# Score columns of the second stage's diagonal blocks: half blocks stacked on the two halves of the partitions

## The chip, the cores and the metric

The kernel runs on one core of a Trainium2 chip. A core has TensorE (PE in the profile; PEld is its weight load), VectorE (DVE), ScalarE (ACT), GpSimd (POOL) and SyncE (SP, which here only issues DMA transfers). They run side by side and meet at semaphores. The metric is the device time of one execution in microseconds (us); lower is better. Matmuls write to PSUM, here eight banks of 512 f32 columns on 128 partitions; DVE and ACT read PSUM, POOL does not.

## What is computed

Two stages, one after the other, on 8 batches of 448 tokens. The first is attention with a soft cap on 12 heads of width 64; its output, laid side by side, is the input x (448 x 768) of the second, four "expert" attentions with a causal mask, of which each token uses two, with weights from a gate. Cut to what matters:

```python
# stage 1, per batch and head
scores = cap * tanh(q @ k.T / 8 / cap)
x[:, head] = softmax(scores) @ v
# stage 2, per batch: 4 experts e, width 64
logits = x @ w_gate                      # the two largest of 4 are kept: w = softmax of the two
s = (x @ wq[e]) @ (x @ wk[e]).T / 8      # keys after the query are masked
out += w[e] * softmax(causal(s)) @ (x @ wv[e]) @ wo[e]
```

## The kernel before

**Stage 1** goes head pair by head pair: 48 pairs p, six to a batch, then two short passes for what is left of the last batch. Scores are held transposed, keys on the partitions. A pair's scores fill three PSUM areas one after the other, named X (three banks X0 to X2) and twice Y (banks Y0, Y1), by matmuls with 64 contraction rows (two heads, one on partitions 0 to 63, one on 64 to 127; `heads`, L854) and one with 128 rows (`tails`, L864). ACT takes each area with tanh (`tanh`, L907) and then the whole pair with exp (`expo`, L919). PE multiplies by the values (`pv`, L934, L942) into one of three banks A0 to A2, DVE normalises (L965, L968) and the result is transposed into xT, the input of stage 2 (L1019 and L1028, later pairs by a DMA transpose).

**Stage 2** of a batch is spread over the pairs of the next batch. `b_v` makes the values vB (L1088, evicted at L1083), `b_qk` queries and keys (L1096), `b_gate` and the functions after it the gate on POOL, `b_mask` the mask of the first or second choice. A half stage is a batch b and a choice s (first or second expert of each token); there are 14 of them, since the last batch has a path of its own (`last`, `last2`). In a half stage:

- `b_score` (L1282) computes the causal scores, all four experts at once: contraction over 2 x 128 rows (r = 0, 1), where the mask leaves a query's row non-zero only at its expert. Keys lie on the 128 partitions in blocks of 128 (block 3 holds only the last 64), queries on the columns. Banks X0 and X1 take 1024 columns: H0 holds the three diagonal blocks of 128 x 128 and two blocks of 64 queries, H1 what lies right of the diagonal. That is 18 matmuls with 128 rows and 128 output partitions.
- One ACT exp over both banks (L1301) writes pB, the probabilities, 1024 columns.
- `causal` (L1308) sets masked entries to zero on POOL: one operation on three diagonal blocks (L1311) and one on the 64 x 64 tail (L1318).
- `b_pv` (L1341) multiplies pB by vB for four query blocks n of 128, ten matmuls of 260 columns (L1351), in PSUM banks from A0 to A2 or X0 to X2, and DVE normalises and weighs the result into oB (L1364, L1366).

After both halves of a batch, `b_ot` adds them on POOL (L1376) and transposes them, for batches from 4 on by a DMA transpose (`turned`, L450 to L454), and `b_wo` multiplies by wo (L1413) and stores the result. The mask of the later batches goes through a DMA transpose as well (mT from mB, L1268, used at L1170).

**What sets the order.** The kernel does not issue as it goes. Each function records operations in a `Graph` with an engine, a cost, reads and writes and, for some, a due time. The order of ACT's fixed operations (tanh and exp) is written out; `solve` lists all others by due time against that clock, and each engine then issues its list in that order. `RANKS` adds hundredths of a us to the due time of single operations from a given planner time on; `TURN` is the planner's time for a DMA transpose, `SWITCH` 0.1 its price when PE goes from or to the matmuls with 64 rows (only operations named sX, sY, sL, sR count as such). Operations with `first` get ahead of others. None of these numbers is an instruction; they move instructions. Where the scores of a half stage come (`exps`), the exp of L1301 stands between two tanh steps of ACT, and the X area of stage 1 must wait for it.

Of the kernel before, what the change touches and what calls it, by code (L numbers as in the profile page):

```python
# [25 lines left out]
    (7.5, {  # L26
        136: 93, 174: 305, 290: -418,
    }),
    (27.5, {
        507: 475,  # L30
    }),
    (67.5, {
        678: -572, 692: 231, 735: -81, 738: -31, 741: 513, 841: 473, 1112: 748, 1167: -284,
    }),
    (87.5, {
        716: 497, 727: -643, 760: -112, 767: -1037, 862: 1282, 888: 375, 919: 264,
    }),
    (127.5, {
        1092: 467, 1196: 214, 1239: -453, 1249: 345, 1267: 323, 1277: 281, 1398: -60, 1401: 289,
        1405: 243, 1449: -132, 1535: 337, 1537: 820,  # L40
    }),
    (147.5, {
        1338: 97, 1345: 117, 1355: 477, 1387: -702, 1413: 186, 1525: 119, 1548: -196,
    }),
    (167.5, {
        1600: 205, 1607: 294,
    }),
# [7 lines left out]
    }),  # L55
    (254.5, {
        2520: -331, 2577: -265, 2635: -902, 2645: 2133, 2659: 128, 2667: 486, 2678: 522, 2702:
        -188, 2703: -340, 2706: -238, 2713: -937, 2729: -581, 2766: 2204, 2788: 297,
    }),
)  # L60
TWIRE = 0.1
TURN = 2.2
SAIL = 1.1
# [11 lines left out]
MD = 4  # L75
# [256 lines left out]
def kernel(  # L332
# [117 lines left out]
    def turned(n, dst, src, r, w, name, due=None):  # L450
# [34 lines left out]
    qm = [[sb(f"qm{s}_{r}", [128, S]) for r in range(2)] for s in range(2)]  # L485
    pP = [sb(f"pP{i}", [128, 2, 64 + 1024]) for i in range(2)]
    pB = [pP[i // 2][:, i % 2] for i in range(4)]
# [15 lines left out]
    qL = sb("qL", [128, 2, 128])  # L503
    vL = sb("vL", [128, E, Dh + 1])
    p2 = yp[NPV % NYP].rearrange("p a s -> p (a s)")[:, 0 : E * 512].rearrange(
        "p (e c t) -> p e c t", e=E, c=4)
# [108 lines left out]
    def setup_b():  # L615
        def pad():
            for t in yf:
                nc.gpsimd.memset(t[:, 7 * S :], 1.0)

        gp(0.5, pad, w=["ypad"], due=120.0)  # L620

        def tri_():
            nc.gpsimd.memset(tri, 0.0)
            for a in range(1, E):
                nc.gpsimd.memset(tri[:, :, a, 0:a], 1.0)

# [10 lines left out]
        def pz():  # L637
            for t in pB:
                nc.gpsimd.memset(t[:, 0:64], 0.0)

        gp(0.6, pz, w=[("pB", i) for i in range(4)])
# [110 lines left out]
    def tr(p):  # L752
# [45 lines left out]
        if p >= KD:  # L798
            pe(0, lambda: tq(g, 0, 2), [("q16", i), "ident"], [("tps", p, "q")], g, occ=0.1,
               name=f"trq{p}")  # L800
            pe(0, lambda: tq(g, 2, 4), [("q16", i), "ident"], [("tps", p, "r")], g, occ=0.1)
            def qe():
# [6 lines left out]
            dve(c_dve(S, p < NAT), qe, [("tps", p, x) for x in "qr"],  # L809
                [("qk", t, "q"), ("qkw", t)], g, name=f"qk{p}")  # L810
            return
# [313 lines left out]
    def b_v(b, ref):  # L1125
        x = b % 2
        j1 = PJ if b == LB - 1 else 0
        for n in range(4):
            g = Group(AUX + XB, 1.8)
            hr = [("half", "v", n)] if b == LB - 1 else []  # L1130
            for j0 in range(j1, NDC, 2):
# [13 lines left out]
                lambda t: t[lo:128, 0 : E * Dh].rearrange("p (e d) -> p e d", d=Dh)),  # L1145
                [("vps", b, n)] + hr, [("vB", x, n)], g, name=f"vB{b}")

    def b_qk(b, ref):
        x = b % 2
        for r in range(2):  # L1150
            for which in "kq":
# [4 lines left out]
                for j in range(j1, NDC):  # L1156
# [3 lines left out]
                               (f"w{which}2", 2 * r), (f"w{which}2", 2 * r + 1)],  # L1160
                       [(which, b, r)], g, name=f"{which}{b}_{r}",
                       due=(ref, 25.225 + 9.62 * r + 13.055 * (which == "q")))
# [80 lines left out]
    def b_mask(b, s):  # L1243
# [9 lines left out]
        if b < MD:  # L1253
            for r in range(2):
# [7 lines left out]

                pe(0, mm, [("mB", s), "ident"], [("mt", b, s, r)], g, occ=0.22, name=f"mT{b}")
                dve(c_dve(S, True), lambda g=g, r=r: nc.vector.tensor_tensor(
# [13 lines left out]
    def keys(c):  # L1278
        o = S - 128 if c == KC else 128 * c
        return slice(o, o + 128)  # L1280

    def b_score(b, s):  # L1282
        x = b % 2
        for part, bk in ((H1, "X1"), (H0, "X0")):
            for i, (o, c, q0, n) in enumerate(part):
                def mm(o=o, c=c, q0=q0, n=n):
                    ps = BANK[f"X{o // 512}"]
                    a = min(n, max(KM - q0, 0))
                    for d, m, t in ((0, a, q0 + TL), (a, n - a, max(q0 - KM, 0))):
                        for r in range(2):  # L1290
                            if m:
                                nc.tensor.matmul(  # L1292
                                    ps[:, o % 512 + d : o % 512 + d + m], kB[x][r][:, keys(c)],
                                    qm[s][r][:, t : t + m], start=(r == 0), stop=(r == 1),
                                )

                pe(0, mm, [("kB", x, r) for r in range(2)] + [("qm", s, r) for r in range(2)],
                   [("s", bk)], occ=2 * c_pe(n), name=f"sB{b}_{s}", takes=(bk,) if i == 0 else ())
        pi = 2 * (b % 2) + s
        pb = pB[pi]  # L1300
        act(c_act(1024), lambda: nc.scalar.activation(  # L1301
            pb[:, 64:], PART["X"].rearrange("p a c -> p (a c)"), AF.Exp, scale=isc),
            [("s", "X0"), ("s", "X1")], [("pB", pi)], fixed=True, name=f"eB{b}_{s}",
            frees=("X0", "X1"))
        b_score.last = fixed_last()
        causal(pb, pi, "")

    def causal(pb, pi, nm):  # L1308
        def diag():
            blk = pb[:, 128:512].rearrange("p (a c) -> p a c", a=3)  # L1310
            nc.gpsimd.affine_select(  # L1311
                out=blk, in_=blk, compare_op=ALU.is_ge, fill=0.0, base=0,
                pattern=[[0, 3], [1, 128]], channel_multiplier=-1,
            )

        def tail():
            blk = pb[64:128, 64:128]
            nc.gpsimd.affine_select(  # L1318
                out=blk, in_=blk, compare_op=ALU.is_ge, fill=0.0, base=0,
                pattern=[[1, 64]], channel_multiplier=-1,  # L1320
            )

        gp(0.6, diag, [], [("pB", pi)], name="diag")
        gp(0.25, tail, [], [("pB", pi)], name="diagt")

    def cols(n):

        res = []
        for c in range(min(n, KC - 1) + 1):
            if c == n:  # L1330
                o = 64 + H0[1 + c][0]
            elif c == 2:
                o = 64 + H0[3][0] + 64
            else:
                o = 64 + H1[c][0] + WIN[n] - 128 * (c + 1)
            res.append((c, o))
        if n == 3:
            res.append((3, 0))
        return res

    def b_pv(b, s):  # L1341
        x = b % 2
        pi = 2 * (b % 2) + s
        for n in range(4):
            g = Group(AUX + XB, 1.6)
            cs = cols(n)
            for i in range(0, len(cs), 2):
                def mm(g=g, i=i, cs=cs):
                    for t in range(i, min(i + 2, len(cs))):
                        c, o = cs[t]  # L1350
                        nc.tensor.matmul(  # L1351
                            bank(g)[:, 0 : E * (Dh + 1)], pB[pi][:, o : o + 128],
                            vB[x][:, c, :, :], start=(t == 0), stop=(t == len(cs) - 1),
                        )

                pe(0, mm, [("pB", pi), ("pB", pi, 0), ("pB", pi, 1), (b, f"mw{s}")] + [("vB", x, c) for c, _ in cs],
                   [("pvB", b, s, n)], g,
                   occ=0.11 * len(cs[i : i + 2]), name=f"pvB{b}_{s}")
            k_ = (2 * s + n) % 4
# [41 lines left out]
    def b_wo(b, ref, off, step=1.0):  # L1401
        x = b % 2
        for n in range(4 if b < LB - 1 else 3):
# [3 lines left out]
            for f in range(2):  # L1407
# [3 lines left out]
                def mm(g=g, n=n, c0=c0, c1=c1):  # L1411
# [447 lines left out]
```

## Time and profile before

| | |
|---|---|
| median of three runs | 305.21 us (304.68 to 305.82) |
| profiled execution, its time | 304.79 us |
| its span in the profile | 303.1 us |
| last two exps of stage 1 on ACT | 283.51 to 286.05 us |
| granted TensorE clock | 1.00 throughout |

Times in the profile are us from the start of its span. A timeline row gives start, length, engine, line, operation, output <- input, partitions x elements and the count of merged instructions. Matmuls overlap: a matmul of 65 columns is shown with 193 ns while the next one starts 30 ns after it. So what PE can do is read from the distance of starts, not from the length of a row.

### The profile page before, as it was taken

How to read it: one execution, taken by the hardware profiler on the slowest of the kernel's cores; microseconds unless marked ns; L12 is line 12 of the kernel's file. 1: busy time of each engine (PE TensorE's matmuls, PEld its weight loads, DVE VectorE, ACT ScalarE, POOL GpSimd, SP SyncE). 2: the span in 40 equal slices, each digit the busy share in tenths (PEclk: the TensorE clock that was granted, in tenths of full speed). 3: DMA queues.
4: the chain of work that ended last, by engine and by line, in shares of the span. 5: the costliest groups of instructions: out<-in, count | busy, mean ns of one | idle time of the engine just before them, and what ended most of it. 6: DMA issues, size and time to landing. Idle time of an engine off the chain costs nothing.

```text
span 303.1 us, 8955 instructions
## 1 busy us (share of the span) xinstructions
PE 282.0 (93%) x3470; PEld 188.1 (62%) x3470; DVE 213.5 (70%) x630; ACT 290.2 (96%) x244; POOL 189.4 (62%) x537
## 2 busy tenths in 40 slices
PE   7897989999999999999999999999898999989992
PEld 4463546666666676667666676656665675657771
DVE  3354556866867877687887887697766878486972
ACT  5999999999999999999999999999999999989981
POOL 6793435997699664958799355927469305711580
PEclk9999999999999999999999999999999999999999
DMA  6999999999993399677996874455028751743136
GB/s 168 223 206 238 236 233 298 284 225 281 264 233 88 118 257 244 161 216 194 280 197 170 235 244 123 55 151 146 2 52 123 216 92 21 103 142 93 37 151 215
DMA packets 86874, 53.12 MB, mean 175 GB/s; under 512 B 47536, under 2 KB 83120, under 8 KB 86832
## 3 DMA queue, kind: packets, MB, share of 16 engines
q1 hardware_dynamic: 86448, 52.13, 69.8%
q8 instruction: 27, 0.44, 0.6%
q10 hardware_dynamic: 384, 0.43, 0.5%
q14 instruction: 15, 0.12, 0.2%
HBM read 36.19 MB, written 11.01 MB: 156 GB/s over the span
## 4 chain that ended last, share of the span: by engine, by line
ACT 64%; PE 15%; POOL 5%; DMA 5%; DVE 5%; issue 4%; ACTq 0%; DVEq 0%; POOLq 0%
ACT yp L907 33%; ACT yp L919 28%; ACT pP L1301 3%; DMA mT<-mB 3%; PE A L1413 2%; PE X L1292 2%; PE A L1088 2%; PE Y L854 1%; DMA ktf<-in_k_dram 1%; PE A L942 1%; POOL oS L1376 1%; POOL mB L1248 1%; PE A L1479 1%; DMA oT<-oS 1%; PE A L1514 1%
## 5 line engine op out<-in xcount | busy, mean ns | idle before, releaser
L919 ACT ACTIVATE yp<-yp 128x3136 f16<-128x3136 f16 (+4 forms) x51 | 142.4, 2794 | 0.0
L907 ACT ACTIVATE yp<-Y 128x896 f16<-128x896 f32 (+2 forms) x100 | 101.7, 1017 | 1.3 <-PE Y L854 1.3
L907 ACT ACTIVATE yp<-X 128x1344 f16<-128x1344 f32 (+2 forms) x50 | 68.3, 1367 | 0.4 <-PE X L854 0.3
L942 PE MATMUL A<-v,yp 128*128 128x65 f16 x1008 | 49.8, 193 | 0.0
L942 PEld LDWEIGHTS <-yp 128*128 128x128 f16 x1008 | 43.6, 97 | 4.0 <-issue 2.1
L934 PE MATMUL A<-vtz,yp 128*128 128x130 f16 x168 | 37.3, 222 | 3.9 <-ACT yp L919 1.6
L744 POOL CAST v<-vf 128x384 f16<-128x384 f32 x48 | 24.6, 519 | 20.8 <-PE A L942 13.1
L968 DVE TENSOR_TENSOR xk<-A,rca 128x256 f16<-128x256 f32 x84 | 35.3, 421 | 2.2
L708 POOL CAST q<-qf 112x512 f16<-112x512 f32 x44 | 26.6, 618 | 13.7 <-PE A L758 9.0
L439 DVE COPY ob<-A 128x384 f32<-128x384 f32 (+1 forms) x50 | 25.6, 550 | 2.4 <-PE A L1413 2.0
L817 DVE COPY qk<-A 128x960 f16<-128x960 f16 x32 | 20.3, 652 | 9.2 <-PE A L758 9.0
L934 PEld LDWEIGHTS <-yp 128*128 128x128 f16 x168 | 16.2, 97 | 16.1 <-issue 8.8
L854 PE MATMUL Y<-qk 64*128 64x448 f16 x136 | 24.7, 357 | 1.5 <-ACT yp L907 0.9
L1366 DVE SCALAR_TENSOR_TENSOR oB<-A,rcb,mw 128x256 f16<-128x256 f32 x55 | 25.3, 477 | 1.0
L1311 POOL TENSOR_SCALAR_AFFINE_SELECT pP<-pP 128x384 f16<-128x384 f16 x14 | 7.4, 528 | 29.3 <-ACT pP L1301 29.3
L965 DVE RECIPROCAL rca<-A 128x4 f32<-128x4 f32 x84 | 15.0, 178 | 14.2 <-PE A L942 13.2
L1413 PE MATMUL A<-wo,oT 128*128 128x384 f16 x106 | 22.8, 326 | 1.0 <-DVE qm L1170 1.0
L1351 PE MATMUL A<-vB,pP 128*128 128x260 f16 x138 | 22.2, 274 | 1.3 <-DVE oB L1366 0.5
L1028 DVE COPY xT<-A 128x448 f16<-128x448 f16 (+1 forms) x38 | 14.7, 386 | 11.2 <-PE A L1019 10.8
L1088 PE MATMUL A<-wvg,xT 128*128 128x260 f16 x168 | 21.3, 274 | 0.6 <-DVE oB L1366 0.3
L1376 POOL TENSOR_TENSOR oS<-oB,oB 128x512 f16<-128x512 f16 x14 | 16.1, 1155 | 8.2 <-issue 5.0
L758 PE MATMUL A<-ident,q 112*128 112x112 f16 x192 | 19.8, 214 | 0.7 <-DVE oB L1366 0.4
(240 smaller groups left out, 620.2 us busy)
## 6 DMA issues: line engine op xcount, KB each, us to landing
qf<-in_q_dram SPq DMA_DIRECT2D x23, 448.0 KB, 5.7
kf<-in_k_dram SPq DMA_DIRECT2D x23, 384.0 KB, 5.0
vf<-in_v_dram SPq DMA_DIRECT2D x23, 384.0 KB, 4.7
out_dram<-ob SPq DMA_DIRECT2D x21, 384.0 KB, 3.1
ktf<-in_k_dram SPq DMA_DIRECT2D x46, 32.0 KB, 5.0
vtf<-in_v_dram SPq DMA_DIRECT2D x46, 32.0 KB, 4.3
out_dram<-ob SPq DMA_DIRECT2D x6, 192.0 KB, 2.9
ob<-in_moe_wv_dram SPq DMA_DIRECT2D x2, 384.0 KB, 4.8
```

The source lines that it names most:

```text
L439: (nc.scalar.copy if o.eng == "ACT" else nc.vector.tensor_copy)(dst(), src())
L708: e(q16[i], qf[s][:, h].rearrange("p h (c d) -> p c h d", c=QC))
L744: nc.gpsimd.tensor_copy(v16[u][:, :, :, 0:Dh], vf[s][:, h].rearrange("p h (c d) -> p h c d", c=KC))
L854: nc.tensor.matmul(dst[:, g, o], kT[r, 128 * (c + 1) : 128 * (c + 2)], t[r, qs], start=True, stop=True,)
L907: ACTS[what, p] = act(c_act(n * (b - a)), lambda: nc.scalar.activation(y[:, a:b, 0:n], src[:, 0 : b - a, 0:n], AF.Tanh, scale=isc / capf), ...
L919: act(c_act(n * (b - a), False), lambda a=a, b=b, n=n: nc.scalar.activation(y[:, a:b, 0:n], y[:, a:b, 0:n], AF.Exp, scale=capf), ks, ks, f ...
L934: nc.tensor.matmul(ps[:, n, :, :], y[:, 2 * S + w : 2 * S + w + 128], vtz[u], start=(n == 0), stop=False, skip_group_check=True,)
L942: nc.tensor.matmul(ps[:, n, h, :], y[:, o : o + 128], v16[u][:, h, c, :], start=False, stop=(c == 2), skip_group_check=True,)
L968: dve(c_dve(128 * m), lambda g=g, i=i, rc=rc, m=m: nc.vector.tensor_tensor(xk[p % NXK][:, 2 * i : 2 * i + m, :, :], view(g)[:, 0:m, :, 0:D ...
L1088: nc.tensor.matmul(bank(g)[:, 0 : E * Dh + E], xT[x][:, j, WIN[n] : WIN[n] + 128], wvg[:, j, :], start=(j == j1), stop=(j == jn),)
L1366: dve(c_dve(E * Dh) + 0.06, lambda g=g, k_=k_, n=n: nc.vector.scalar_tensor_tensor(oB[s][:, n, :, :], view(g)[:, :, 0:Dh], rcb[k_][:, 0, : ...
L1413: nc.tensor.matmul(bank(g)[:, 0 : D // 2], oT[x][:, n // 2, r, n % 2, :], wo2[r][:, c0:c1], start=(r == 0), stop=(r == 1),)
```

## The change

The diagonal blocks of 128 x 128 are no longer computed whole. A diagonal block has three quarters that matter: the two triangles of 64 x 64 on its diagonal and the full square above them. The square and one triangle need all keys of the block for its later 64 queries (they become part of `ROWS`, 128 partitions). The triangle of the earlier 64 queries needs only 64 keys (`HALF`): two such half blocks share 64 columns, one on output partitions 0 to 63, one on 64 to 127. Scores take 2 x 448 columns in place of 2 x 512.

```diff
-    H0 = ((0, KC, KM, 64), (64, 0, 0, 128), (192, 1, 128, 128), (320, 2, 256, 128),
-          (448, 2, KM, 64))
-    H1 = ((512, 0, 128, 320), (832, 1, 256, 192))
+    HALF = ((0, 0, 0, 0), (0, 64, KM, KM), (448, 0, 256, 256), (448, 64, 128, 128))
+    ROWS = ((64, 0, 64, 384), (512, 1, 192, 256), (768, 2, 320, 128))
...
+        its = [[("r", *y) for y in ROWS if y[0] // 448 == i] + [
+            ("h", *y) for y in HALF if y[0] // 448 == i] for i in range(2)]
+        for i in (1, 0):
+            for m_, (kind, o, c, q0, n) in enumerate(its[i]):
+                lead = m_ == 0
+                if kind == "h":
+                    row, k0, q0, n = slice(c, c + 64), q0, n, 64
+                    kk = slice(k0, k0 + 64)
+                else:
+                    row, kk = slice(0, 128), slice(128 * c, 128 * (c + 1))
...
+                    ps = PART["X"][row, i, o - 448 * i : o - 448 * i + n]
...
-        act(c_act(1024), lambda: nc.scalar.activation(
-            pb[:, 64:], PART["X"].rearrange("p a c -> p (a c)"), AF.Exp, scale=isc),
+        act(c_act(896), lambda: nc.scalar.activation(
+            pb.rearrange("p (a c) -> p a c", a=2), PART["X"][:, 0:2, 0:448], AF.Exp, scale=isc),
```

The causal mask takes three POOL operations in place of two, and the zeroed columns of pB with their four memsets go:

```diff
+        gp(0.28, lambda: keep(two[0:64, :, 0:64], [0, 2], [1, 64]), [], [("pB", pi)], name="diag")
+        gp(0.42, lambda: keep(two[64:128, :, 0:128].rearrange("p a (b c) -> p a b c", b=2),
+                              [0, 2], [0, 2], [1, 64]), [], [("pB", pi)], name="diag")
+        gp(0.2, lambda: keep(pb[64:128, 768:832], [1, 64]), [], [("pB", pi)], name="diagt")
```

The product with the values is split accordingly. A query block n below 3 gets, in place of one matmul for its diagonal block, one with 64 rows into output partitions 0 to 63 and one with 128 rows into 64 to 127; block 3 ends with one of 64 rows into 64 to 127. For n = 1 the half block lies on partitions 64 to 127 while its values lie on 0 to 63, so a DMA copies them into a new buffer vH once for each batch. The banks are now A0 to A2 alone.

```diff
+            if n == 1:
+                sp(lambda: nc.sync.dma_start(vH[x][64:128], vB[x][0:64, 1]), [("vB", x, 1)], [("vH", x)],
+                   name=f"vH{b}", lat=2.6)
...
+    def own(n):
+        return ((0, 0), (64, 448), (0, 448))[n]
...
-            g = Group(AUX + XB, 1.6)
+            g = Group(AUX, 1.6)
+            its = []
+            for c in range(min(n, KC)):
+                o = ROWS[c][0] + WIN[n] - ROWS[c][2]
+                its.append((slice(0, 128), slice(o, o + 128), slice(0, 128), vB[x][:, c]))
+            if n < KC:
+                p0, o = own(n)
+                v_ = vH[x] if n == 1 else vB[x][:, n]
+                its.append((slice(p0, p0 + 64), slice(o, o + 64), lo64, v_))
+                o = ROWS[n][0]
+                its.append((slice(0, 128), slice(o, o + 64), hi64, vB[x][:, n]))
+            else:
+                its.append((hi64, lo64, hi64, vB[x][:, n]))
...
+                        nc.tensor.matmul(
+                            bank(g)[q_, 0 : E * (Dh + 1)], pb[rows, cs], v_[rows],
+                            start=(t == 0 or len(its) == 2), stop=(t >= len(its) - 2),
+                            skip_group_check=True)
```

The planner's numbers are new: `TURN`, and a `RANKS` list of 35 tables in place of 9, most of them new. Some buffers that an eviction waited for are now named by the matmul before it, so that the planner lists that matmul later.

```diff
-TURN = 2.2
+TURN = 3.0
 RANKS = (
...
-                   [("wop", b, n, f)], g, occ=0.325, name=f"wo{b}")
+                   [("wop", b, n, f), ("ob", n, f)], g, occ=0.325, name=f"wo{b}")
...
-                   [("pvB", b, s, n)], g,
-                   occ=0.11 * len(cs[i : i + 2]), name=f"pvB{b}_{s}")
+                   [("pvB", b, s, n)] + [("rcb", (2 * s + n) % 4)] * (i == 0), g,
+                   occ=0.11 * len(its[i : i + 2]), name=f"pvB{b}_{s}")
...
```

The order of ACT's fixed operations is the same in both kernels. On the other engines the order differs from the first 20 us on. In the built programs PE has 3470 matmuls before and 3540 after; SP has seven more transfers (the copies to vH) and the same number of every other kind.

More of the change, by code (lines that the diff above doesn't have):

```diff
@@ new lines @@
+    (233.43, {
+        2252: -705, 2336: 300, 2398: 1708, 2521: 339, 2530: 192, 2582: 57, 2607: 262, 2665: 503,
+        2669: 334, 2696: -310,
+    }),
+    (83.5, {
+        608: 378, 689: 206,
+    }),
+    (189.5, {
+        1743: 794, 1831: 339,
+    }),
+    (203.5, {
+        1759: 351, 1776: 1390, 1948: 179, 2182: -495,
+    }),
+    (217.5, {
+        2160: 326,
+    }),
+    (231.5, {
+        2252: 620, 2451: 412, 2471: 180,
+    }),
+    (245.5, {
+        2328: 1111,
+    }),
+    (214.5, {
+        1776: -364, 1945: 353, 2006: 293, 2008: 240, 2051: 118, 2069: -356, 2160: 340, 2212:
+        785, 2341: 456, 2396: -451, 2471: -308, 2521: 489,
+    }),
@@ L485 @@
     qm = [[sb(f"qm{s}_{r}", [128, S]) for r in range(2)] for s in range(2)]
[L486 removed]
+    pP = [sb(f"pP{i}", [128, 2, 896]) for i in range(2)]
     pB = [pP[i // 2][:, i % 2] for i in range(4)]
@@ L504 @@
     vL = sb("vL", [128, E, Dh + 1])
+    vH = [sb(f"vH{i}", [128, E, Dh + 1]) for i in range(2)]
     p2 = yp[NPV % NYP].rearrange("p a s -> p (a s)")[:, 0 : E * 512].rearrange(
@@ L1160, in b_qk @@
                                (f"w{which}2", 2 * r), (f"w{which}2", 2 * r + 1)],
-                       [(which, b, r)], g, name=f"{which}{b}_{r}",
+                       [(which, b, r)] + ([("qm", s, r) for s in range(2)]
+                                          if which == "q" and b >= MD else []), g, name=f"{which}{b}_{r}",
                        due=(ref, 25.225 + 9.62 * r + 13.055 * (which == "q")))
```

161 lines of the change are left out of this document (92 added, 69 removed), and 13 rows, old and new, of the table RANKS.

## The prediction

> **What bounds the kernel now.** I read the page's totals first, then the waits of ACT and its timeline, then the same for PE, and last the chain.
>
> ```profile
> PE 282.0 (93%) x3470; PEld 188.1 (62%) x3470; DVE 213.5 (70%) x630; ACT 290.2 (96%) x244; POOL 189.4 (62%) x537
> ```
> ```profile
> ACT yp L907 <- PE Y L854: 1.3, 1, 1.3
> ...
> ACT pP L1301 <- PE X L1292: 0.9, 1, 0.9
> ACT yp L907 <- PE X L854: 0.3, 1, 0.3
> ```
>
> ACT is busy 96%. Once it runs (its first wait, 1.3, is at the start) it waits twice, 1.2 us together, until the last exp of stage 1. What a step of ACT costs is the distance of starts:
>
> ```profile
> 212.16 2.84 ACT L919 ACTIVATE yp<-yp 128x3136 f16<-128x3136 f16 x1
> 214.87 1.05 ACT L1301 ACTIVATE pP<-X 128x1024 f16<-128x1024 f32 x1
> 215.77 0.95 ACT L907 ACTIVATE yp<-Y 128x896 f16<-128x896 f32 x1
> 216.57 1.34 ACT L907 ACTIVATE yp<-X 128x1344 f16<-128x1344 f32 x1
> ```
>
> The score exp of 1024 columns takes 0.90 us (214.87 to 215.77), a tanh over two slices of 448 columns 0.80 us. But ACT is not alone. Windows of the whole middle, of one pair of heads, and of the end (columns: length, then busy time and count of PE, PEld, DVE, ACT, POOL, then clock, DMA share, GB/s):
>
> ```profile
> 62.00:279.00 217.00, 208.55 (x2631) 142.56 (x2631) 164.38 (x478) 215.71 (x169) 139.63 (x356) 1.00 0.66 163
> ```
> ```profile
> 85.00:90.49 5.49, 5.49 (x70) 3.67 (x71) 3.30 (x9) 5.49 (x5) 5.49 (x16) 1.00 0.88 239
> ```
> ```profile
> 279.00:303.10 24.10, 18.29 (x235) 12.87 (x234) 15.68 (x56) 16.16 (x30) 10.66 (x36) 1.00 0.38 126
> ```
>
> In the middle PE is idle for 8.45 of 217 us, in the pair shown not at all, and there ACT is full as well. So both engines are near their limit, and the question is how much PE has to spare. Its timeline around that pair:
>
> ```profile
> 84.72 0.35 PE L1096 MATMUL A<-xT,wk 128*128 128x448 f16 x1
> 85.00 0.36 PE L854 MATMUL Y<-qk 64*128 64x448 f16 x2
> 85.20 0.35 PE L854 MATMUL X<-qk 64*128 64x448 f16 x2
> 85.49 0.34 PE L1019 MATMUL A<-perm,xk 128*128 128x128 f16 x3
> 85.67 0.22 PE L1019 MATMUL A<-pswap,xk 128*128 128x128 f16 x1
> 85.72 0.54 PE L1096 MATMUL A<-xT,wk 128*128 128x448 f16 x2
> 86.10 0.61 PE L1351 MATMUL A<-vB,pP 128*128 128x260 f16 x4
> ...
> 88.23 0.34 PE L942 MATMUL A<-v,yp 128*128 128x65 f16 x6
> 88.51 0.36 PE L854 MATMUL Y<-qk 64*128 64x448 f16 x2
> 88.81 0.23 PE L934 MATMUL A<-vtz,yp 128*128 128x130 f16 x1
> ```
>
> Three things stand here. (1) Two matmuls of 64 rows on the two partition halves cost one: each L854 row is a pair, and the X pair ends 0.19 after the Y pair (85.55 after 85.36), the step of 448 columns. Steps fit columns / 2.4 GHz + 2.5 ns throughout. (2) A change from matmuls with 128 rows to such with 64 or back costs 0.105 us: L1096 ends at 85.07, the pair of 448 columns after it at 85.36, which is 0.29 and not 0.19; L942 ends at 88.57, L854 at 88.87, 0.30; back to 128 rows, the first L1019 (0.22 long) ends at 85.71, 0.16 after 85.55, where 0.055 is its step. (3) PE fills a score area as soon as ACT has freed it, so it can be late by little: the Y pair of 88.51 ends at 88.87, and ACT takes it at 89.21.
>
> ```profile
> 88.04 1.53 ACT L907 ACTIVATE yp<-X 128x1344 f16<-128x1344 f32 x1
> 89.21 1.17 ACT L907 ACTIVATE yp<-Y 128x896 f16<-128x896 f32 x1
> ```
>
> **PE's load in the middle.** I cut 62 to 279 us at the end of each first fill of an X area, 38 stretches, 216.6 us. The 2631 matmuls of the window row come to 174.8 us by the step formula (pairs of 64 rows once), the 180 changes between 128 and 64 rows at 0.105 to 18.9 us: 193.7 in all, so 23.0 us to spare (8.45 of it visible as idle; the rest lies behind the overlap of rows). It is uneven: stretches of a half stage's score have 0.6 to 2 us, those of `b_v` and `b_qk` next to none (80.0 to 85.6: 5.53 of 5.59 us).
>
> **The change, part by part.** *ACT's exp over 896 columns.* 0.90 becomes 0.80, as the tanh over the same two slices of 448: 14 x 0.105 = −1.47 us on ACT. That an access of two slices costs more than one run is excluded by that same row.
>
> *More matmuls.*
>
> ```profile
> L1351 PE MATMUL A<-vB,pP 128*128 128x260 f16 x138 | 22.2, 274 | 1.3 <-DVE oB L1366 0.5 <-DVE qk L817 0.2
> ...
> L1292 PE MATMUL X<-qm,kB 128*128 128x64 f16 x112 | 10.8, 193 | 0.2 <-DVE qm L1170 0.2
> L1292 PE MATMUL X<-qm,kB 128*128 128x128 f16 x112 | 10.6, 220 | 0.0
> ...
> L1351 PE MATMUL X2s<-vB,pP 128*128 128x260 f16 x2 | 0.4, 274 | 0.0
> ```
>
> A half stage's product with the values has 13 matmuls in place of ten; four take 0.61 with 0.274 for the last, so 0.112 each: +0.34 us, 4.7 us in all. Its scores have 20 in place of 18 with the same column sum (8 x 64 + 2 x 768 against 2 x 1024), and small ones cost by columns (193 against 220 ns for 64 more): 0. Two of 140 products lay outside A0 to A2, so banks A alone cost nothing.
>
> *New array shapes.* This the planner does not know: its price of 0.1 is for sX, sY, sL, sR alone. A half stage had one shape, 128 rows x 128 output partitions; now it has 128 x 64 (score halves; the late rows of a diagonal block) and 64 x 64 (the products of half blocks). Scores: whole, halves, whole, halves, whole: 4 changes, all of output width. Products: 3 each for n = 0, 1, 2 (into 64 x 64, to 128 x 64, back) and 2 for n = 3: 11, of which 8 change the rows and 3 only the width. In the two built orders shapes change 240 times before and 429 times after (340 counting rows alone). No row shows a change of width. From below it is 0: going to 112 rows and back costs nothing.
>
> ```profile
> 136.09 0.33 PE L768 MATMUL A<-ident,k 128*128 128x128 f16 x3
> 136.26 0.26 PE L758 MATMUL A<-ident,q 112*128 112x112 f16 x2
> ```
>
> (L768 ends at 136.42, the two L758 at 136.52: 0.05 each.) The nearest row is L854, whose halves lie at partitions 0 and 64 of the array as the new ones do, and it pays 0.105; I take that for every change of shape. The Trainium skill, TensorEngine Tiling (Array Packing), section Tiling Modes, says that a change of tiling mode, not just of tile, drains the TensorE, and it lists 128 x 64 and 64 x 64 as modes of their own; by it the width counts as the rows do, and the sum is the one I take; by rows alone it would be that of the second rival. The trace agrees for the rows (0.105) and shows nothing for the width.
>
> In the middle PE then needs 178.5 us of steps and, with every change of shape, 37.6 of changes: 216.0, for 215.1 us that ACT takes after the saving. It no longer fits. Stretch by stretch the need beyond ACT's time sums to 9.1 us if nothing carries over; if PE may be late by 0.2, 0.5, 0.7 us before ACT waits (0.34 stood between fill and use above, more where exp gives cover), 7.6, 5.5, 4.1. Two examples: 80.0 to 85.6 needs 6.46 of 5.59 (12 more L1096 and two more products moved there, two more changes); 242.7 to 251.0 needs 9.83 of 8.20. I take 5.5; bounds 4.1 and 9.1. ACT stands still for that long; behind each late fill wait the tanh, the exp of the pair and its products.
>
> *Later transfers.* ACT's one long wait had a late transpose behind it:
>
> ```profile
> 260.37 5.33 DMA mT<-mB
> 265.73 0.64 DVE qm L1170
> 266.40 0.49 PE A L1413 x2
> 266.89 0.45 PE X L1292 x8
> ```
> ```profile
> mT<-mB SPq DMA_TRANSPOSE x6, 4.0
> ```
>
> 5.33 us where 4.0 is the median; then DVE, PE and the exp, 0.85 late, and 0.33 after it. An order that counts on 0.8 us more puts other work first. Between 0 and −1.18; I take −0.6, since PE is the later one in much of the new order.
>
> *POOL and the copy to vH.*
>
> ```profile
> L1311 POOL TENSOR_SCALAR_AFFINE_SELECT pP<-pP x14: 522/527/535, 70.2 to 278.2; 128x384 f16<-128x384 f16 x14
> L1318 POOL TENSOR_SCALAR_AFFINE_SELECT pP<-pP x14: 237/238/240, 70.8 to 278.8; 64x64 f16<-64x64 f16 x14
> L1585 POOL TENSOR_SCALAR_AFFINE_SELECT pP<-pP x6: 407/410/416, 287.3 to 290.9; 128x256 f16<-128x256 f16 x6
> ```
> ```profile
> SPq L1427 <- DVE ob L439: 21.7, 16, 7.5
> ```
>
> Mask: 0.77 us before; after, 128, 256 and 64 columns, some 0.29 + 0.41 + 0.24 = 0.94. The 0.17 lies beside stage 1's PE work, since the products come over 3 us after the exp; uncovered, it is 14 x 0.17 = 2.4. The seven copies wait at SP's head for an eviction, and the loads stand behind them; SP already stands 7.5 us at a store and no load is late for it, and the copy is read four or five pairs later. 0, up to 0.3 each without that cover. The four memsets gone lie at 20 us beside idle POOL: 0.
>
> *The end.* After 279 PE is busy 18.29 of 24.10 us. The order leaves it 1.1 us more of steps after the last X fill (three products, four L1413, one L1514) and 8 to 11 changes, 0.8 to 1.2: between 0 and +2.3; most lies beside ACT's last exps, so +0.6.
>
> **Sum**, on the profiled 304.79: −1.47 + 5.5 − 0.6 + 0.6 = +4.0, **308.8 us**. The median of the three runs is 0.42 higher; I add nothing for it. Own range: −1.47 −1.18 + 4.1 gives 306.2, −1.47 + 9.1 + 2.3 gives 314.7.
>
> **Rivals.** (1) *The new shapes are free.* PE then needs 197.4 − 1.7 (changes of L854 that fall beside a half block) = 195.7 of 215.1, no stretch is over by more than 0.5, and ACT keeps its saving: 304.79 − 1.47 − 0.6 = 302.7, faster. For it: a half block uses one part of an array whose rest stays as it was. Against it: L854 is just that and pays. At 0.07 a change the stalls are about 1.5 us and with the end eat the saving; from there it is slower. (2) *Only rows count, the width does not.* 207.0 of 215.1 us; over by 4.3 without carry, 1.2 with 0.5: 304.79 − 1.47 − 0.6 + 1.2 + 0.4 = 304.3, up to 307.5. (3) *Lateness feeds itself:* products come late, banks A with them, DVE and POOL behind, and the masks' transposes start later, so that each of the last four batches adds a wait like the one at 266: 308.8 + 4 x 1.2 = 313.6. For it, DVE's waits are all on PE; against it, PE is late by less than 1 us at a time.
>
> **How the numbers follow.** Forecast 0.58, rival 1 0.17, rival 2 0.20, rival 3 0.05. 0.5% (1.5 us), about what a measurement of this kernel can tell from no change, puts the borders at 303.7 and 306.7. Faster: rival 1 nearly whole and a third of rival 2, 0.22. Same: most of the rest of rival 2 and the edges, 0.14. Slower 0.64. The range runs from 303.0, into rival 1, to 312.5: below it lies about 0.1, above it 0.1 of the forecast's far end and rival 3.
>
> **What would show it.** Score exps 0.80 apart from the next tanh: the first term. After a matmul of 64 x 64 or 128 x 64, the next whole one ends 0.105 beyond its step: the second; if it ends on its step, rival 1. ACT waits <- PE Y and X L854 that sum to 4 to 8 us, in stretches such as 80 to 86 and 242 to 251, with PE busy 99% there. No wait of the exp at 266. The prediction is wrong if ACT stays at 96% or more and its waits on PE stay near 1 us.

## The result, and the profile after

The changed kernel takes 316.59 us (median of four runs, 315.84 to 317.7) where the kernel before takes 305.07 beside it: a ratio of 1.0377 (1.034 to 1.0415). The profiled execution is the slowest of the four, with a span of 316.0 us for 303.1. The page's totals and the chain of waits, by engine, after:

```profile
PE 298.8 (95%) x3540; PEld 191.3 (61%) x3540; DVE 218.1 (69%) x628; ACT 292.3 (93%) x246; POOL 192.3 (61%) x547
...
PE 75%; ACT 18%; DVE 4%; DMA 1%; issue 1%; POOL 0%; SPq 0%; DVEq 0%
```

and the same chain before:

```profile
ACT 64%; PE 15%; POOL 5%; DMA 5%; DVE 5%; issue 4%; ACTq 0%; DVEq 0%; POOLq 0%
```

ACT was 96% busy and set the end; now PE does. ACT's longest waits, after (total, times, longest):

```profile
ACT yp L983 <- PE Y L930: 4.4, 10, 1.3
ACT pP L1386 <- PE X L1378: 3.7, 3, 1.7
ACT yp L983 <- PE X L930: 2.4, 5, 0.7
```

Before, the same three rows were 1.3, 0.9 and 0.3; in the first row the 1.3 of before and 1.8 of the 4.4 after fall into the first 11 us. L930 is the line that was L854, L1378 the scores of stage 2 (L1292 before), L1386 their exp. Two windows with both engines, before and then after (busy time and count of PE, PEld, DVE, ACT, POOL):

```profile
62.00:131.00 69.00, 66.99 (x866) 46.71 (x868) 50.36 (x150) 69.00 (x53) 54.25 (x143) 1.00 0.79 205
242.00:279.00 37.00, 34.60 (x437) 23.26 (x434) 27.18 (x79) 35.80 (x34) 12.25 (x31) 1.00 0.45 94
```
```profile
62.00:131.00 69.00, 68.04 (x833) 44.66 (x832) 48.77 (x142) 67.68 (x50) 50.62 (x137) 1.00 0.84 216
242.00:279.00 37.00, 36.73 (x429) 22.59 (x427) 29.99 (x81) 34.08 (x31) 16.04 (x45) 1.00 0.53 117
```

PE is busy longer in the same time while it gets through fewer matmuls (833 for 866, 429 for 437): its time goes into something that is not work.

**Where the 12.9 us of span are.** I cut each execution at two rows of ACT: the second tanh over X (1344 columns), and the last exp of stage 1 (the first and the last row below, before and then after).

```profile
9.40 1.29 ACT L907 ACTIVATE yp<-X 128x1344 f16<-128x1344 f32 x1
...
283.51 2.54 ACT L919 ACTIVATE yp<-yp 128x1920 f16<-128x1920 f16 x2
```
```profile
11.10 1.29 ACT L983 ACTIVATE yp<-X 128x1344 f16<-128x1344 f32 x1 [0.68 <-PE X L940]
...
288.09 0.92 ACT L1386 ACTIVATE pP<-X 128x896 f16<-128x896 f32 x1 [1.58 <-PE X L1378]
...
294.32 2.56 ACT L995 ACTIVATE yp<-yp 128x1920 f16<-128x1920 f16 x2
```

Start 9.40 to 11.10, +1.7. Middle, from there to the end of the last exp: 286.05 − 9.40 = 276.7 before, 296.88 − 11.10 = 285.8 after, +9.1. Tail, from there to the end of the span: 17.0 and 19.1, +2.1. The start isn't the change's: an experiment below (`last_half`) has the changed kernel's order up to 255 us and starts at 9.22.

In the middle the distance from each fixed step of ACT to the next, above the usual one of its kind (the tenth of a hundred, ordered by length), adds up to this:

| us beyond the usual step | before | after |
|---|---|---|
| tanh steps of the pairs wait | 2.3 | 9.2 |
| score exps of stage 2 wait | 1.2 | 4.5 |

+7.0 and +3.3, with 0.25 on other exps, less the 1.47 that the shorter exp saves: +9.1, the whole of the middle. The pair that the prediction showed at 88 us, after, on ACT and then on PE:

```profile
84.88 1.30 ACT L983 ACTIVATE yp<-X 128x1344 f16<-128x1344 f32 x1
86.17 0.92 ACT L983 ACTIVATE yp<-Y 128x896 f16<-128x896 f32 x1
86.99 2.81 ACT L995 ACTIVATE yp<-yp 128x3136 f16<-128x3136 f16 x1
89.69 0.91 ACT L983 ACTIVATE yp<-Y 128x896 f16<-128x896 f32 x1
90.49 1.29 ACT L983 ACTIVATE yp<-X 128x1344 f16<-128x1344 f32 x1
91.86 0.92 ACT L983 ACTIVATE yp<-Y 128x896 f16<-128x896 f32 x1
```
```profile
85.77 0.36 PE L930 MATMUL Y<-qk 64*128 64x448 f16 x2
...
91.45 0.36 PE L930 MATMUL Y<-qk 64*128 64x448 f16 x2
```

The fill of Y ends at 86.13 and ACT takes it at 86.17; at 91.81 and 91.86 in the next pair. Before, 0.34 stood between; now the cover is gone and the step from X to the second Y takes 1.29 and 1.37 where it took 1.17. Such steps from X to Y are late by more than 0.03 us 16 times, 4.8 us in all, some of them by too little for the wait rows; before, none is.

### The profile page after: what moved, and what is told of

It reads as the page before. It is cut to its first block, busy times and chain, and to the rows that moved or that the text cites. A ratio compares the mean times of both kernels' runs of the same rounds, so it can differ in the third digit from the quotient of the medians.

```text
span 316.0 us, 9120 instructions
## 1 busy us (share of the span) xinstructions
PE 298.8 (95%) x3540; PEld 191.3 (61%) x3540; DVE 218.1 (69%) x628; ACT 292.3 (93%) x246; POOL 192.3 (61%) x547
## 4 chain that ended last, share of the span: by engine, by line
PE 75%; ACT 18%; DVE 4%; DMA 1%; issue 1%; POOL 0%; SPq 0%; DVEq 0%
PE A L1432 10%; ACT yp L983 9%; PE A L1172 9%; ACT yp L995 9%; PE A L1018 7%; PE Y L930 7%; PE A L1494 6%; PE A L1164 5%; PE X L1378 5%; PE A L1010 4%; PE X L940 3%; PE X L930 3%; PE A L1095 2%; PE A L834 2%; PE A L844 2%; DMA qf<-in_q_dram 1%
## 5 line engine op out<-in xcount | busy, mean ns | idle before, releaser
L995 ACT ACTIVATE yp<-yp 128x3136 f16<-128x3136 f16 (+4 forms) x51 | 137.6, 2700 | 0.0
L983 ACT ACTIVATE yp<-Y 128x896 f16<-128x896 f32 (+2 forms) x100 | 92.3, 923 | 4.6 <-PE Y L930 4.4
L983 ACT ACTIVATE yp<-X 128x1344 f16<-128x1344 f32 (+2 forms) x50 | 64.1, 1282 | 3.2 <-PE X L930 2.4
L784 POOL CAST q<-qf 112x512 f16<-112x512 f32 x44 | 27.0, 626 | 18.5 <-PE A L834 12.9
L1432 PE MATMUL A<-vB,pP 128*128 128x260 f16 (+2 forms) x168 | 37.4, 286 | 0.2
L1432 PEld LDWEIGHTS <-pP 128*128 128x128 f16 (+2 forms) x182 | 17.0, 101 | 20.1 <-issue 11.5
L930 PE MATMUL Y<-qk 64*128 64x448 f16 x136 | 25.1, 364 | 3.5 <-ACT yp L983 3.3
L1447 DVE SCALAR_TENSOR_TENSOR oB<-A,rcb,mw 128x256 f16<-128x256 f32 x56 | 26.6, 481 | 2.5 <-POOL oS L1457 0.4
L1395 POOL TENSOR_SCALAR_AFFINE_SELECT pP<-pP 64x128 f16<-64x128 f16 (+2 forms) x42 | 12.7, 317 | 21.7 <-ACT pP L1386 12.8
L769 POOL CAST k<-kf 128x384 f16<-128x384 f32 x33 | 16.3, 508 | 8.1 <-PE A L844 6.5
```

Source lines behind the costliest of these rows:

```text
L784: e(q16[i], qf[s][:, h].rearrange("p h (c d) -> p c h d", c=QC))
L930: nc.tensor.matmul(dst[:, g, o], kT[r, 128 * (c + 1) : 128 * (c + 2)], t[r, qs], start=True, stop=True,)
L983: ACTS[what, p] = act(c_act(n * (b - a)), lambda: nc.scalar.activation(y[:, a:b, 0:n], src[:, 0 : b - a, 0:n], AF.Tanh, scale=isc / capf), ...
L995: act(c_act(n * (b - a), False), lambda a=a, b=b, n=n: nc.scalar.activation(y[:, a:b, 0:n], y[:, a:b, 0:n], AF.Exp, scale=capf), ks, ks, f ...
L1432: nc.tensor.matmul(bank(g)[q_, 0 : E * (Dh + 1)], pb[rows, cs], v_[rows], start=(t == 0 or len(its) == 2), stop=(t >= len(its) - 2), skip_ ...
L1447: dve(c_dve(E * Dh) + 0.06, lambda g=g, k_=k_, n=n: nc.vector.scalar_tensor_tensor(oB[s][:, n, :, :], view(g)[:, :, 0:Dh], rcb[k_][:, 0, : ...
```

## The experiments

Theory A: the changes of shape fill PE, and ACT waits for what PE lacks. Theory B, in the first four: the new order, later transfers, POOL's third operation and the copies to vH cost the time, whatever the shapes. The other runs name their rivals.

A change of shape below is a change between matmuls that use different rows or output partitions of the array, other than 128 rows to 112 and back. "Need" is the sum, over the 38 stretches of the prediction, of what PE's steps and changes take beyond ACT's time, with the prices measured in the trace after, less the 1.47 of the shorter exp; in the old forms there is no saving to subtract. Where two products of 260 columns follow each other in the two column halves of the array, the second is counted at the 0.004 us that the traces of `own_rows128` and `before_split` show for it; the figure in brackets counts it whole, as the expectations of these two runs did. All rows: middle and tail cut as above, profiled run; median, and ratio to the kernel before, which took 304.52 to 305.49 us beside them.

| kernel | changes | need, nothing carried | middle, against before | tail | tanh waits / score waits | median | ratio |
|---|---|---|---|---|---|---|---|
| before | 240 | 0.0 | 0 | 17.0 | 2.3 / 1.2 | 305.07 | |
| changed | 429 | 8.5 | +9.1 | 19.1 | 9.2 / 4.5 | 316.59 | 1.0377 |
| `all_whole` | 242 | −0.8 | −0.7 | 18.6 | 2.0 / 2.3 | 305.98 | 1.0028 (1.0007 to 1.0049) |
| `pv_whole` | 287 | 0.4 | +1.9 | 18.5 | 3.5 / 3.4 | 307.93 | 1.0105 (1.0066 to 1.0144) |
| `sc_whole` | 386 | 6.6 | +6.5 | 19.1 | 8.3 / 2.9 | 314.08 | 1.0306 (1.0267 to 1.0345) |
| `own_rows128` | 392 | 3.2 (5.5) | +4.7 | 18.6 | 5.9 / 3.7 | 311.18 | 1.0186 (1.0156 to 1.0216) |
| `before_split` | 329 | 1.5 (4.3) | +1.4 | 17.3 | 3.8 / 1.0 | 307.31 | 1.0075 (1.0041 to 1.0109) |
| `before_turn3` | 238 | 0.0 | +3.4 | 18.9 | 3.7 / 3.2 | 308.95 | 1.0111 (1.0059 to 1.0164) |
| `last_half` | 425 | 8.0 | +8.6 | 19.2 | 10.6 / 2.6 | 315.72 | 1.0362 (1.0341 to 1.0384) |

**Whole shapes in the new order.** Three kernels keep the changed kernel's order, columns and count of matmuls, and give the halves the whole array, in the scores and the products, in the products alone, in the scores alone; they compute other sums.

```diff
-                    row, k0, q0, n = slice(c, c + 64), q0, n, 64
-                    kk = slice(k0, k0 + 64)
+                    row, k0, q0, n = slice(0, 128), q0, n, 64
+                    k0 = min(k0, S - 128)
+                    kk = slice(k0, k0 + 128)
...
-                its.append((slice(p0, p0 + 64), slice(o, o + 64), lo64, v_))
+                its.append((slice(0, 128), slice(o, o + 128), slice(0, 128), vB[x][:, n]))
...
```

> The changed kernel's operations, counts and order as they are, but every score half and every product on the whole 128 x 128 array: the split products take all 128 rows and columns and the score halves all 128 keys, so the output is not the reference's. Shape changes fall from 429 to 242, two more than before. Theory A (the drains at shape changes fill PE): PE's need in the middle falls from 217 to 197 us of 215, so ACT keeps its saving: 304.9 us, between 303.5 and 306.5. Theory B (the new order, the later transfers, POOL's third operation or the copies to vH cost the time): still 315 to 317, since all of these stay.

> Only the products on the whole array (142 shape changes fewer), the score halves stay at 128 x 64; output not the reference's. Theory A: need 202 us, 1.9 us beyond ACT's time stretch by stretch, less the saving of 1.5: 306.5 us, between 305 and 308. Theory B: 315 to 317.

> Only the score halves on the whole array (43 shape changes fewer), the products stay split into 64 x 64 and 128 x 64; output not the reference's. Theory A: need 212 us, 8.1 beyond ACT's time: 314 us, between 312.5 and 315.5; both effects together give that of all_whole. Theory B: 315 to 317.

305.98, 307.93 and 314.08: of the 10.6 us between whole shapes and the changed kernel the products' shapes alone bring 8.1 (144 more changes) and the score halves alone 1.95 (45 more); the last 0.55 comes only with both. The new order, the later transfers, three mask operations and the copies to vH are all in `all_whole`, and its middle is 0.7 below the kernel before. But its tail is 1.5 longer, so that nothing is won even with the shapes at no price.

**One part in the old order.** The kernel before with each diagonal product split by output width, nothing else changed:

```diff
+                        for q_ in (0, 64) if c == n else (None,):
+                            qs = slice(0, 128) if q_ is None else slice(q_, q_ + 64)
...
```

> The kernel before, in its own order, with exp over 1024 columns and no half blocks; only the product of each diagonal block is made in two matmuls of 128 x 64, one per output half: 3 more matmuls and some 6 more shape changes in a half stage, which its planner does not know (329 changes in place of 240), same result. Theory A: need 209 us, 4.3 beyond ACT's time stretch by stretch although 8 us stay free in the sum: 309.8 us, between 308 and 311.5. Theory B, or PE's 23 us to spare taking it up: 305 to 306.

Neither: 307.31. The shapes cost here too, and its score exps wait no more than before. The middle grew by 1.4 where the expected need was 4.3, but that sum counted every half product whole. In the trace the two halves of a product run side by side:

```profile
79.88 0.41 PE L1353 MATMUL A<-vB,pP 128*64 128x260 f16 x4
```

The four halves of two products take 0.41; four matmuls of this length one after the other took 0.61. With that the need is 1.5, and the middle shows nearly all of it, so no cover is seen here. (The edit makes four more matmuls in a half stage, not three, since the 64 x 64 block is split as well.)

**One shape fewer in the products.** The half blocks' products over all 128 rows and 64 output partitions:

```diff
-                its.append((slice(p0, p0 + 64), slice(o, o + 64), lo64, v_))
+                its.append((slice(0, 128), slice(o, o + 64), lo64, vB[x][:, n]))
...
```

> The changed kernel, but the products of the half blocks read all 128 rows (of another 64 keys too, so the sums are others; for that three of four diagonal blocks add products of keys that do not belong to them) and stay 64 output partitions wide: as many matmuls and columns as the changed kernel, but one array shape (128x64) where it has two, 392 changes of shape in the order in place of 429. Theory A (each change of shape empties the array for 0.10 to 0.12 us, and the middle of the kernel has none of it to spare): the need beyond ACT's time falls by 3.0 us, from 8.5 net to 5.5: 313.6; if halves in the two column halves also run side by side, down to 311. Range 310.5 to 314.3. Rival (what costs is the number of small matmuls and the order, not the changes): 316.6 as the changed kernel, 316 to 317.5.

311.18, at the low end. PE's timeline shows why the low end:

```profile
75.91 0.30 PE L1432 MATMUL A<-vB,pP 128*64 128x260 f16 x2
76.14 0.34 PE L844 MATMUL A<-ident,k 128*128 128x128 f16 x3
```

Two products in the two column halves take the 0.30 of one. Count of matmuls and order are those of the changed kernel; only shapes differ, and 5.4 us went. The need falls by 5.3: 3.0 by the 37 changes that are gone, 2.3 by products side by side.

**The order alone.** The kernel before with the planner's price of a transfer at 3.0, as in the change:

```diff
-TURN = 2.2
+TURN = 3.0
```

> The kernel before with nothing but the planner's price for a transfer raised from 2.2 to 3.0 as in the change: old instructions, another order. Theory A (the order costs only what it adds in changes of shape and in PE's work after the last X fill; 238 changes for 240, 0.5 us more of work in the tail): 305.6, 304.5 to 306.4. Rival (counting on later transfers by itself makes the end longer, which would be the 1.5 us that the tail of the changed order with whole shapes has more): 306.5 to 307.5.

308.95, above the rival too. PE's need is zero, yet the middle is 3.4 and the tail 1.9 longer. But 2.5 of the 3.4 lie ahead of 62 us, in two waits: 1.2 at 15.9, behind a load that took 7.45 us, and 1.3 at 34.8, where the granted TensorE clock of the profiled execution was 0.50 (the last three figures are clock, DMA share and GB/s):

```profile
28.60:35.40 6.80, 6.31 (x50) 3.79 (x51) 3.37 (x9) 5.69 (x5) 1.45 (x4) 0.50 1.11 253
```

The second goes with the lower clock; whether the order caused either is open. Two of the four executions, with a mean clock of 0.994 and 0.999, took 308.03 and 307.88, still above the rival. In the 38 stretches the order costs 0.9 in all. ACT and PE around the longest wait there:

```profile
237.13 2.97 ACT L919 ACTIVATE yp<-yp 128x3136 f16<-128x3136 f16 x1
242.31 1.02 ACT L1301 ACTIVATE pP<-X 128x1024 f16<-128x1024 f32 x1 [2.21 <-PE X L1292]
```
```profile
239.34 0.81 PE L1413 MATMUL A<-wo,oT 128*128 128x384 f16 x4
239.99 0.92 PE L1292 MATMUL X<-qm,kB 128*128 128x64 f16 x10
240.75 0.22 PE L934 MATMUL A<-vtz,yp 128*128 128x130 f16 x1
...
241.71 0.50 PE L1292 MATMUL X<-qm,kB 128*128 128x128 f16 x8
```

The last eight of the exp's matmuls stand behind four pairs of L934 and L942, 0.96 of the 2.21 us. The list in `RANKS` came with the price of 2.2; under another price it shifts the same operations among others. So the run doesn't say what a fitted order at 3.0 would cost.

**Other lists.** `old_planner` is the changed kernel under the old `TURN` and `RANKS`, `a_noranks` the changed kernel with

```diff
...
+RANKS = ()
```

and `told_noranks` that kernel with the changes of shape added to the planner's lengths of the score halves and products.

> The changed kernel's instructions under the old settings of the planner (the old price of a transfer and the old list of shifted ranks). 411 changes of shape, PE's need in the middle 214.6 us, beyond ACT's time by 9.7 net of the exp's saving if nothing carries over and by 6.8 if PE may be late by 0.5 us; 2.9 us more work of PE after the last X fill than before. Theory A (need stretch by stretch decides, whatever the order): 313 to 317.5, near 315.5. Rival (the new order is what costs, the new shapes alone cost about what the split products did in the old order, 2.2 us, and as much again for the scores): 308 to 311.

> The changed kernel without its list of shifted ranks, the planner's price of a transfer at 3.0. 401 changes of shape, PE's need in the middle 212.8 us, beyond ACT's time by 5.1 net; 4.4 us more work of PE after the last X fill than before. Theory A (need by stretch and the tail decide): middle about +5, tail +2 to +4.4: 312 to 315, a little under the changed kernel. Rival (the list of ranks, found without a price for the new changes of shape, is still what keeps the order good): 317 or more.

> The changed kernel without its list of shifted ranks, and with the planner told the price of the changes of shape in the lengths of the score halves and of the products (0.11 to 0.33 us each); to be compared with the run without the list and without the price, 320.7. 391 changes for 401, PE's need in the middle 210.6 for 212.8 us, but over ACT's time by 9.4 net stretch by stretch for 5.1, and 1.1 us more work after the last X fill. Theory A (the need of each stretch beyond ACT's time sets the middle): 4 to 5 us longer than the run without the price, 323 to 327. Rival (the sum of need over the whole middle sets it, and an honest price makes a better order): 2 us shorter or more, 316 to 319.

323.47, 320.68 and 325.06 (ratios 1.0603, 1.0501, 1.0681). The first two lie above what need gives: their middles are 14.2 and 9.8 longer than before where need was 9.7 and 5.1, and the 4 to 5 us above it are a few long waits, of up to 6.1 and 3.5 us; in `old_planner` the granted clock was also 0.50 from 273.8 to 277.2. `a_noranks` lies where its rival had it: without the list the order is worse. `RANKS` names operations by their number, and the old list hits other operations in the new kernel, so `old_planner` tests a list that fits nothing. The third is to be read against the second: middle +3.8 (need +4.3), tail +0.9. The sum of need over the middle had fallen by 2.2 us; the stretches that were over decided. ACT's longest waits there:

```profile
ACT pP L1270 <- PE X L1262: 13.0, 5, 3.7
```

The score exps wait 7.1 us more than in `a_noranks` and the tanhs 3.0 less. That the longer score halves in the planner pushed the exps back is likely, but not shown.

**The score exps' waits.** `last_half` puts the last score half of a half stage directly behind the one before it, which alters PE's order in two places.

```diff
+    for nm in dict.fromkeys(o.name for o in order if o.name[:2] == "sB"):
+        its = [o for o in order if o.name == nm]
+        at = order.index(its[-2])
+        order.remove(its[-1])
+        order.insert(at + 1, its[-1])
```

> The changed kernel with PE's order altered in two places and nowhere else: the last score half of a half stage (four matmuls of 64 columns) stands directly behind the half before it, in the two places where other work stood between (the last stage but one, whose exp waits 1.84 us at 259, and the last, whose exp waits 1.68 us at 288; there 7 products of stage 3's projections stood ahead). 425 changes of shape for 429. Theory A (PE is full in the middle, so its work is only exchanged there; the waits of the exp before the very end, where PE has idle time, can be had): 0.4 to 0.5 us for four changes and up to 1.0 at 288, so 315.4, 314.8 to 316.2, with the exp's wait at 259 replaced by waits of the tanh that follow. Rival (the exps' waits are a loss of their own beside PE's load): both waits fall by 0.7 to 1.1 and nothing takes their place: 314.4 to 315.0. Rival (the wait only moves to the tail): 316.6, 316.2 to 317.2.

315.72. Its ACT rows, where the changed kernel waited 1.58 at 288.09:

```profile
284.68 0.92 ACT L1386 ACTIVATE pP<-X 128x896 f16<-128x896 f32 x1 [0.36 <-PE X L1378]
285.50 0.80 ACT L983 ACTIVATE yp<-Y 128x768 f16<-128x768 f32 x1
287.19 1.13 ACT L983 ACTIVATE yp<-X 128x1152 f16<-128x1152 f32 x1 [0.89 <-PE X L930]
```

The score exps wait 1.9 less, the tanhs 1.4 more, 0.89 of it in the second step behind. The middle is 0.5 shorter, what the four changes are worth. While PE is full, ACT's waits on it were moved here and, but for this, not removed. (The two ratios, 1.0362 and 1.0377, lie inside each other's intervals; the waits carry this reading.)

**A repair.** `repaired` takes the products of `own_rows128` against copies of the values padded with zeros, and the order of `last_half`; it computes what the changed kernel computes.

```diff
-                sp(lambda: nc.sync.dma_start(vH[x][64:128], vB[x][0:64, 1]), [("vB", x, 1)], [("vH", x)],
+                    nc.sync.dma_start(vH[x][0:64, 0], vB[x][0:64, 0])
+                    nc.sync.dma_start(vH[x][64:128, 1], vB[x][0:64, 1])
+                    nc.sync.dma_start(vH[x][0:64, 2], vB[x][0:64, 2])
...
```

> The changed kernel's sums by other means: the products of the half blocks read all 128 rows against copies of the values whose other 64 rows are zero (three copies per batch in place of one, made by transfers from SP), and the last score half stands directly behind the half before it. One shape less, 387 changes of shape or a few more for 429. Theory A: as the run of the half products on 128 rows, 311.2, less up to 1 us for the last halves, plus up to 0.5 us for two more transfers in SP's queue: 310.8, 309.8 to 312. Rival (the added copies land late or hold up SP's loads, so that products or pairs wait): 313 or more.

312.93 (1.0278, 1.0232 to 1.0323): faster than the changed kernel, 0.9% slower than `own_rows128`, between the two expectations. Its middle waits 2.21 and 2.42 where `own_rows128` waits 0.35 and 1.64:

```profile
250.78 0.70 ACT L984 ACTIVATE yp<-Y 128x640 f16<-128x640 f32 x1 [2.21 <-PE Y L931]
251.38 2.81 ACT L996 ACTIVATE yp<-yp 128x3136 f16<-128x3136 f16 x1
256.61 0.92 ACT L1391 ACTIVATE pP<-X 128x896 f16<-128x896 f32 x1 [2.42 <-PE X L1383]
```

The chain leads from the first back over PE's products to an eviction that waited 1.25 for a store, which SP issued at 242.54, behind two transposes that had held its queue for 3.51; in `own_rows128` three stores left at 240.76. SP's order differs by more than the copies, so that the copies caused it is not shown. And after PE had stood still for part of 245.4 to 247.8, the granted clock was 0.50 until 251.3:

```profile
245.40:247.80 2.40, 1.35 (x10) 0.71 (x10) 1.86 (x5) 2.40 (x3) 0.00 (x0) 1.00 1.06 179
247.95:251.30 3.35, 3.35 (x23) 1.54 (x22) 2.30 (x7) 1.14 (x2) 0.00 (x0) 0.50 0.97 312
```

So part of the 2.21 us, an estimated 1.3 by the steps of these matmuls at full clock, is the lower clock of the profiled execution.

## Why the prediction was wrong, point by point

The sign and the mechanism were right: new shapes fill PE, and ACT, which set the end before, waits for it. The size was not: +4.0 forecast, +11.5 between medians, above the range and above the 314.7 of the forecast's own bounds.

**ACT's exp, −1.47: right.** Two rows of the trace after, a score exp and the next tanh, are 0.80 apart:

```profile
106.54 0.94 ACT L1386 ACTIVATE pP<-X 128x896 f16<-128x896 f32 x1
107.34 0.95 ACT L983 ACTIVATE yp<-Y 128x896 f16<-128x896 f32 x1
```

**The price of a change, 0.105 for rows and width alike: nearly right.** PE after, at 81 us:

```profile
81.27 0.27 PE L1432 MATMUL A<-vB,pP 128*128 128x260 f16 x1
81.47 0.29 PE L1432 MATMUL A<-vH,pP 64*64 64x260 f16 x1
81.70 0.34 PE L1095 MATMUL A<-perm,xk 128*128 128x128 f16 x3
81.88 0.22 PE L1095 MATMUL A<-pswap,xk 128*128 128x128 f16 x1
82.03 0.30 PE L1432 MATMUL A<-vB,pP 128*64 128x260 f16 x1
```

The ends are 81.54 and 81.76: 0.22 for a step of 0.112, so 0.11 to enter 64 x 64. From 82.10 to 82.33: 0.23, so 0.118 to enter 128 x 64, where only the width changes. Over all such pairs it is 0.114 into 64 x 64, 0.117 to 0.118 into 128 x 64, and 0.103 to 0.106 into the other shapes. That settles rivals 1 and 2: the shapes are not free, and the width counts as much as the rows. The Trainium skill, TensorEngine Tiling (Array Packing), section Tiling Modes, says that a change of tiling mode drains the TensorE. The trace agrees in that such a change costs time, 0.118 us for a change of width alone. At the measured prices PE's need is 217.2 us for the 216.0 of the prediction, and need beyond ACT's time, nothing carried, 9.95 instead of 9.1.

**What a full PE costs ACT, 5.5: the step that failed.** The prediction let PE be late by about 0.5 us before ACT waits, from a fill 0.34 ahead of its use "more where exp gives cover". That took 9.1 us of need down to 5.5. The runs show no such cover. In the changed kernel ACT waits 10.6 us more in the middle, all of it in the 38 stretches, where need with nothing carried is 9.95 at the measured prices. Less the exp's 1.47, the middles of `sc_whole`, `all_whole` and, in the old order, `before_split` come within 0.1 of that need, and none of the kernels lies further below it. The others lie 0.6 to 4.7 above: the changed kernel and `last_half` 0.6, `pv_whole` 1.4, `own_rows128` 1.5, those with another list or other copies most. So need with nothing carried was the least that the new shapes cost, and it stood in the prediction as the upper bound, 9.1.

The 10.6 are of two kinds. The tanhs wait 7.0 more, 4.8 of it at the second Y of each pair. A cover of 0.35 counted once would give 7.3 for all tanhs of the changed kernel, but only 0.1 for `before_split`, where they grew by 1.4; so that agreement is no rule. The score exps, for which I had set no wait of their own, wait 3.3 more: the last matmuls of the two longest stand behind other work in PE's fixed order, as `last_half` shows. Why the cover does not help, and what the excess above need is made of in each kernel, is shown only in part: score waits grow by 1.1 in the new order even with whole shapes and not at all in `before_split`.

**Later transfers, −0.6: not seen as a gain.** The wait at 266 is gone, but score exps wait longer in every kernel of the new order, 2.3 in `all_whole` for 1.2.

**POOL and the copy to vH, 0: agrees.** Both are in `all_whole`, whose middle is below that of before by half of the exp's 1.47; the other half is those 1.1 us of score waits, less 0.3 on the tanhs.

**The end, +0.6 of 0 to 2.3: too small.** It was +2.1. 1.5 is the order's, with whole shapes too. The other 0.55 goes with the products' shapes: it is there in `sc_whole` (19.1) and not in `pv_whole` (18.5). The work that the order left past the last X fill does not hide beside ACT's last exps.

**Rival 3**, lateness that feeds itself: score exps in the last batches did wait 1.84, 0.5 and 1.68 us, but the two long ones in good part behind other work in PE's queue: `last_half` takes them from 1.84 to 1.13 and from 1.68 to 0.46.

## What to carry to other kernels

Count the changes of array shape in the built order before splitting matmuls into parts of the array: here 189 more changes, 0.103 to 0.118 us each, put some 20 us on an engine that had 23 to spare in all but not in each stretch, to save 1.5 us on another. When two engines are both near full, size a loss stretch by stretch with no cover, take the sum as the least loss, and give the waits behind a fixed order a term of their own. Look at the granted clock in each stretch before a wait is put down to the order. A list of shifts fitted to one set of operations is part of the kernel: under another price or another set of operations the kernel was longer by 2.4 us and more.

## What was not expected of the hardware

The price of a change depends on the shape that is entered (0.105, 0.114, 0.118), not only on that something changes. And two products of 260 columns with 128 rows, in the two column halves, run side by side like the two row halves of L930: the second ends some 5 ns after the first (0.107 of its 0.112 is gone), while score halves of 64 columns gain 15 to 23 ns of their 29 by it. `before_split` has the same overlap at all its split products, so that its half products cost the changes of shape and little else.
